# A linear-attention and rational-FFN kernel: the third token tile goes through three quarters of the inner units ahead of the last quarter of the first two

## The chip, the core and the metric

The kernel runs on one core of a Trainium2 chip. The metric is the time of one execution in device microseconds, as the median of several runs. An execution's span, from its first to its last instruction, is what the profiler shows; the time is a little longer than the span.

## What is computed

```python
# linear attention, 4 x 8 heads, 768 steps, 48 wide
for t in range(S):
    cur = einsum('bhd,bhe->bhde', u * k[t], v[t])
    y[t] = einsum('bhd,bhde->bhe', r[t], state + cur)
    state = w[None, :, :, None] * state + einsum('bhd,bhe->bhde', k[t], v[t])
x = y.transpose(0, 2, 1, 3).reshape(3072, 384)
# feed-forward, 384 -> 2048 -> 384, with a rational activation
h = x @ w_in
P = a[0] + a[1] * h + a[2] * h**2 + a[3] * h**3
Q = 1 + |b[0]| * |h| + |b[1]| * h**2
out = (P / (Q + 1e-6)) @ w_out
```

`r`, `k`, `v` are float32; the weights `w_in` (384 x 2048) and `w_out` (2048 x 384) come as float64 and are turned into float32 on the chip.

## The kernel before, in words

**Tiles.** The 3072 tokens are 24 blocks of 128, block n being time chunk n // 4 of batch n % 4. Two blocks are a pair in the attention and a token tile of 256 in the feed-forward: 12 tiles. The 2048 inner units are 16 pieces j of 128. A *slice* s is one tile with two neighbouring j (`JG`), so eight slices are a tile; slices are numbered in the order in which they run, by the list `SL`.

**One slice.** TensorE makes `h` (`f1`, L644: three float32r products, high with high, low with high, high with low; for tile 0 alone, `FULL`, one float32 product per chunk, L650). ScalarE (ACT) makes |h| (L692), two squares (L698, L703), a logarithm (L708) and an exponential (L712), which is 1/Q. VectorE (DVE) makes P's first factor (L716), the high part of the activation (L722), and two steps towards its low part (L726, L732); the low part's product `lo` (L736) is done by GpSimd (POOL) or by DVE, which for the first 20 slices the order table says (`DYN`). Then TensorE multiplies high and low parts with `w_out` into `o` (`f2`, L654 to L656), 12 matmuls a slice.

**Weights.** The weights are 28 pieces (12 of `w_in`, named `i<quarter>_<chunk>`, 16 of `w_out`, named `o<j>`). SP loads a piece's raw words (L374) into one of few staging buffers; ACT does a copy (L392) and two more steps (L380, L383), DVE joins them (L397, out `wfi` or `wfo`), the high part is a cast (L420, `whii`, `whio`), the remainder (L417, `wloi`, `wloo`) is made by POOL or DVE. A quarter of the inner units, four j, needs three pieces of `w_in` and four of `w_out`. Tile 0 reads `wf`, so a remainder of `w_in` is made once tile 0 is through with that quarter.

**Attention.** For a pair, POOL and DVE scale `k` and `r` (L486, L490) and make the bonus (L494 to L508), TensorE transposes (`tk`, `tr`, L513), makes `kv` (L562), `a` (L541) and `y` (L591), DVE masks (`av`, L549), sums the state (L573) and adds `y` (L607). Then `x` is transposed (L619), copied to `xth` (L420) and its remainder made, `xtl` (`xt_lo`, L633).

**What sets the order.** Every step is a task in a table that `build()` and `prologue()` fill; the string `ORDER` lists the tasks by number in the order in which they are issued, each with the letter of its engine where there is a choice (P, D, A, G, S for TensorE, DVE, ACT, POOL, SP), and `w1` is a warming matmul. Each engine runs its own part of this list strictly in order. `placed()` walks through it with the counts of buffers in `CAP`.

**The quarters.** In the kernel before, `NT` = 2 and `NSEG` = 4: tiles 0 and 1 take turns by quarter, (0, first), (1, first), (0, second) and so on, 16 slices; then tile 2 and all later tiles run through whole. At the end of each quarter of tiles 0 and 1 the partial sum in `o` is taken out (`put_out`: the first by L783 or L785 into a buffer `os`, the later ones added to it by DVE, L778), since one `o` per half is all there is.

**The head.** `prologue()` loads `w` (`wraw`), which after two ACT steps (L304, L305) goes through DVE's power scan (L312), and the coefficients `a`, `b`, which take ACT's L260, L261, L265 and L266 and DVE's L264 and L267 to L290, short steps that all activation steps need.

Of the kernel before, what the change touches and what calls it, by code (L numbers as in the profile page):

```python
# [31 lines left out]

PRM = {'NT': 2,
 'NSEG': 4,
# [10 lines left out]
234 0 35 12 13 14 16 18 15 17 20 19 21 5 4 7 22 23 27 44 45 46 47 58 233 59 60 61 1 10 24 25 3 243 30 28 48 236G 11 238G 239 6  # L45
244 62 241 242 29 51 246 245 248G 255 256 26 52 53 54 31 63A 253 254 w1 260 w1 37 38 39 36 55 250G 237G 249G 251 w1 40 262 235
240G 247 259 257A 264A 261 156 157 258A 158 159 41 252G 42D 265 263 267 56D 160 161D 269 268 270 79 80 81 82 83 84A 276 277 279G
280D 285 273 272 271D 274 86 87 275D 88 89 90 2 8 9 72 73 65 66 74 281G 287 85G 64G 266G 282G 289 290 292G 295G 67 75 49A 76 68
69 286D 70D 71G 789 790 791 288D 283 77D 793 93 94 792 803 804 293G 294G 291 278 304 43G 284G 95 794 796 296 96 795 97 797 798
799 800G 309D 805 128 129 130 807 131 132 806 w1 324 100 101 808 102 103 298 300 301D 310 299D 810 104 801 802 78G 323 326G 329G  # L50
297G 327G 114 107 809 115 116 117 303A 811 812 813 814G 305 307 306 308 328D 108 302A 109 110 133A 118 119A 111 312 313 319 314
815 334 318 315 332 336 325 337 339G 342G 343 121 122 123 124 335A 333A 226 227 338 316D 320 321A 317 125 126A 228 340G 345 346D
341G 347 348D 149 150 322 330 351 356 352 229 230 151 816A 152 135 136 137 57G 50G 819 820 821 112D 357 354 98D 153 91D 105D 353
355 138 139 822 154D 823 826 817 818D 824 825 827 828 829 170 350S 171 349S 833 834 837 127G 113G 331G 359 360 361 172 835 173
174 344G 849 850 836 838 365 840 140D 366 212 213 863 864 384 466 142 830G 831 839 841 842 843 99D 832 844D 845 847 851 214 852
215 216 854 865 853 856 855 857 858 848D 143 866 144 868 106G 92G 120G 162G 859 860G 145 146 846D 867 870 147D 869 871 872 385
# [104 lines left out]
def tile_linear_attention_rational_ffn(ctx, tc, r, k, v, w, u, w_in, w_out, a, b, out):  # L161
# [19 lines left out]
    NV = 5  # L181
    TR = HALF + D
    RAW = PRM["RAW"]
    NT = PRM["NT"]
    FULL = PRM["FULL"]
    FULL2 = PRM["FULL2"]
    NTC = 2
# [478 lines left out]
    def opens(s):  # L666
        f, j0, _ = SL[s]
        return j0 == 0 or (f < NT and NT > 1 and j0 % SEG == 0)
# [420 lines left out]
```

## Time and profile before

| | us |
|---|---|
| median of three runs | 544.45 |
| the three runs | 544.45, 541.43, 544.65 |
| the profiled execution | 542.21 |
| its span | 540.4 |
| PE busy | 510.0 (94%) |
| DVE busy | 427.9 (79%) |
| ACT busy | 404.5 (75%) |
| POOL busy | 250.0 (46%) |
| mean granted clock of TensorE | 0.991 |

PE is TensorE's matmuls, DVE is VectorE, ACT is ScalarE, POOL is GpSimd, SP issues the DMAs. "Busy" is the time in which at least one of the engine's instructions was under way; matmuls overlap, so a busy PE need not be at its peak. A row's waits name the engine that was released and the one that released it. A line number is that of the kernel before.

### The profile page before, as it was taken

Reading aid. Unit: us, or ns where it says so; the run is one execution under the profiler, and the core shown is the slowest. Engines: PE = TensorE matmul, PEld = TensorE weight load, DVE = VectorE, ACT = ScalarE, POOL = GpSimd, SP = SyncE. Lnnn points to the kernel's source line nnn. Section 1 sums busy time; section 2 is a strip of 40 time slices with the busy share of each in tenths; the row PEclk is TensorE's granted clock in tenths of the full one; section 3 lists DMA queues with packets and bytes.
Section 4 is the critical chain, followed back from the end, with each engine's and each line's share of the span. In section 5 each row is a group of like instructions: output and inputs, shape, how many; then the busy total and the mean of one; then the engine's idle time right before and its main releaser. Section 6 shows DMA issues by size and latency. Waiting matters only on the chain.

```text
span 540.4 us, 14734 instructions
## 1 busy us (share of the span) xinstructions
PE 510.0 (94%) x6055; PEld 490.7 (91%) x6055; DVE 427.9 (79%) x708; ACT 404.5 (75%) x666; POOL 250.0 (46%) x241
## 2 busy tenths in 40 slices
PE   4758999899999999999999999999999999999995
PEld 2647988899999999999999999999999899999995
DVE  5889999899974887887796868789867785776872
ACT  5789999998864857948963857876785785788782
POOL 3669545384444662551563654235523432222331
PEclk9899999999999999999999999999999999999999
DMA  8967642240022311104304232040031000000001
GB/s 205 267 172 202 183 112 76 79 80 16 16 52 50 79 32 45 31 4 89 81 2 91 52 76 52 2 81 2 2 82 32 1 30 2 2 30 1 29 2 35
DMA packets 88492, 33.46 MB, mean 62 GB/s; under 512 B 81761, under 2 KB 84834, under 8 KB 88418
## 3 DMA queue, kind: packets, MB, share of 16 engines
q1 hardware_dynamic: 88418, 32.46, 25.4%
q8 instruction: 49, 0.80, 0.6%
q14 instruction: 25, 0.20, 0.1%
HBM read 27.73 MB, written 4.72 MB: 60 GB/s over the span
## 4 chain that ended last, share of the span: by engine, by line
PE 76%; DVE 5%; ACT 4%; DMA 1%; issue 1%; POOL 0%; DVEq 0%; POOLq 0%; ACTq 0%; SPq 0%
PE h L644 30%; PE o L654 11%; PE o L656 11%; PE o L655 11%; PE y L591 3%; PE h L650 2%; PE kv L562 2%; PE a L541 2%; PE tr L513 2%; PE tk L513 2%; PE x L619 1%; DVE q L726 1%; DVE g L722 1%; ACT w L698 1%; DVE h L716 1%
## 5 line engine op out<-in xcount | busy, mean ns | idle before, releaser
L736 POOL TENSOR_TENSOR g<-q,z 128x512 fp32r<-128x512 f32 (+1 forms) x92 | 118.5, 1289 | 234.4 <-DVE q L732 142.9
L644 PE MATMUL h<-xth,whii 128*128 128x256 f32 x528 | 151.2, 286 | 0.1
L644 PE MATMUL h<-xtl,whii 128*128 128x256 f32 x528 | 148.0, 280 | 0.0
L644 PE MATMUL h<-xth,wloi 128*128 128x256 f32 x528 | 148.0, 280 | 0.0
L654 PE MATMUL o<-whio,g 128*128 128x384 f32 x384 | 134.5, 350 | 0.0
L656 PE MATMUL o<-whio,g 128*128 128x384 f32 x384 | 130.3, 339 | 1.9 <-DVE g L736 1.9
L655 PE MATMUL o<-wloo,g 128*128 128x384 f32 x384 | 129.9, 338 | 0.0
L698 ACT ACTIVATE w<-q,off,root 128x512 f32<-128x512 f32 (+1 forms) x97 | 75.4, 779 | 48.5 <-DVE q L726 22.5
L644 PEld LDWEIGHTS h<-xth,whii 128*128 128x128 f32 x528 | 99.4, 188 | 1.7 <-DVE q L726 0.9
L644 PEld LDWEIGHTS h<-xtl,whii 128*128 128x128 f32 x528 | 99.5, 188 | 0.0
L644 PEld LDWEIGHTS h<-xth,wloi 128*128 128x128 f32 x528 | 99.4, 188 | 0.0
L722 DVE SCALAR_TENSOR_TENSOR g<-h,sig,z 128x512 fp32r<-128x512 f32 (+1 forms) x97 | 72.1, 743 | 33.7 <-ACT z L712 29.2
L716 DVE SCALAR_TENSOR_TENSOR h<-t,sig,h 128x512 f32<-128x512 f32 (+1 forms) x97 | 71.9, 743 | 15.6 <-ACT t L703 9.7
L703 ACT ACTIVATE t<-h,off,root 128x512 f32<-128x512 f32 (+1 forms) x97 | 74.3, 767 | 6.8 <-PE h L644 6.6
L726 DVE SCALAR_TENSOR_TENSOR q<-w,sig,g 128x512 f32<-128x512 f32 (+1 forms) x97 | 72.2, 744 | 6.3
L656 PEld LDWEIGHTS o<-whio,g 128*128 128x128 f32 x384 | 72.1, 188 | 3.2 <-DVE g L736 2.9
L732 DVE SCALAR_TENSOR_TENSOR q<-h,sig,q 128x512 f32<-128x512 f32 (+1 forms) x97 | 72.0, 744 | 2.7
L654 PEld LDWEIGHTS o<-whio,g 128*128 128x128 f32 x384 | 72.1, 188 | 1.0
L655 PEld LDWEIGHTS o<-wloo,g 128*128 128x128 f32 x384 | 72.3, 188 | 0.1
L692 ACT ACTIVATE q<-h 128x512 f32<-128x512 f32 (+1 forms) x97 | 56.2, 584 | 20.7 <-PE h L644 19.7
L712 ACT ACTIVATE z<-z,lnb 128x512 f32<-128x512 f32 (+1 forms) x97 | 69.7, 719 | 2.2
L708 ACT ACTIVATE z<-w,lnb 128x512 f32<-128x512 f32 (+1 forms) x97 | 66.0, 680 | 6.9 <-POOL g L736 2.6
(141 smaller groups left out, 664.9 us busy)
## 6 DMA issues: line engine op xcount, KB each, us to landing
sti<-in_moe_w_in_dram SPq DMA_DIRECT2D x12, 512.0 KB, 5.1
sto<-in_moe_w_out_dram SPq DMA_DIRECT2D x16, 384.0 KB, 3.8
rh<-in_r_dram SPq DMA_DIRECT2D x24, 192.0 KB, 3.5
kh<-in_k_dram SPq DMA_DIRECT2D x24, 192.0 KB, 4.0
vn<-in_v_dram SPq DMA_DIRECT2D x24, 192.0 KB, 4.4
out_dram<-os SPq DMA_DIRECT2D x24, 192.0 KB, 2.1
vo<-in_v_dram SPq DMA_DIRECT2D x10, 96.0 KB, 3.9
wraw<-in_w_dram SPq DMA_DIRECT2D x1, 1.0 KB, 2.5
```

What stands on the lines that cost most here:

```text
L644: nc.tensor.matmul(o, w_[nm][:, c], x_[:, cc], start=(n == 0), stop=(n == 3 * NCC - 1))
L654: nc.tensor.matmul(o, hi, w_["hi"], start=first, stop=False)
L655: nc.tensor.matmul(o, hi, w_["lo"], start=False, stop=False)
L656: nc.tensor.matmul(o, lo, w_["hi"], start=False, stop=last)
L698: nc.scalar.activation(g["w"], w_, AF.Square, scale=RB, bias=KB)
L703: nc.scalar.activation(g["t"], g["h"], AF.Square, scale=RA, bias=KA)
L712: nc.scalar.activation(g["z"], g["z"], AF.Exp, scale=-1.0, bias=lnb[:, 1:2])
L716: nc.vector.scalar_tensor_tensor(g["h"], g["t"], KAP, g["h"], op0=ALU.add, op1=ALU.mult)
L722: nc.vector.scalar_tensor_tensor(g["hi"], g["h"], c0, g["z"], op0=ALU.add, op1=ALU.mult)
L726: nc.vector.scalar_tensor_tensor(g["q"], g.get("w", g["q"]), qe, g["hi"].bitcast(F32), op0=ALU.add, op1=ALU.mult)
L732: nc.vector.scalar_tensor_tensor(g["d"], g["h"], c0, g["q"], op0=ALU.add, op1=ALU.subtract)
L736: e.tensor_mul(g["lo"], g["d"], g["z"])
```

## The change

`NT` and `NSEG` go, and a list of groups comes in their place: (tile, first quarter, end quarter). Tiles 0 and 1 take turns in the first three quarters (12 slices), then tile 2 runs through the same three quarters in one group (slices 12 to 17), then tiles 0, 1 and 2 each through the last (18 to 23). From tile 3 on all is as it was. Tile 2's sum is therefore taken out twice instead of once. `xth` has three buffers and `xtl` two, where both had two, and `xtl` is made only when it is first written. The order table is written anew for the whole program, from its first task on; so the engines' queues differ in many places, the choice of DVE or POOL included.

```diff
-PRM = {'NT': 2,
- 'NSEG': 4,
+PRM = {'GROUPS': ((0, 0, 1), (1, 0, 1), (0, 1, 2), (1, 1, 2), (0, 2, 3), (1, 2, 3), (2, 0, 3), (0, 3, 4), (1, 3, 4), (2, 3, 4)),
...
 ORDER = """
-234 0 35 12 13 14 16 18 15 17 20 19 21 5 4 7 22 23 27 44 45 46 47 58 233 59 60 61 1 10 24 25 3 243 30 28 48 236G 11 238G 239 6
+0 156 157 w1 7 35 12 13 14 16 15 w1 18 17 20 51 158 159 52 160 3 6 5 4 22 23 27 19 21 w2 29 24 1 25 30 161D 162G 2 245 8 9 53 54
...
+    NXT = {"xth": 3, "xtl": 2}
...
     def xt_lo(n):
         f, q = divmod(n, TB)
+        if q == 0:
+            xts[f].append(at.tile([P, NCC, N1], F32R, tag="xtl", name=f"xtl{f}", bufs=NXT["xtl"]))
...
-    NSEG = PRM["NSEG"]
-    SEG = NJ // NSEG
-    SL = [(f, j, JG) for g in range(NSEG) for f in range(NT) for j in range(g * SEG, (g + 1) * SEG, JG)] if NT > 1 else []
-    SL += [(f, j, JG) for f in range(NT if NT > 1 else 0, NTILE) for j in range(0, NJ, JG)]
+    SEG = NJ // 4
+    PART = [(f, a * SEG, b * SEG) for f, a, b in GROUPS]
+    PART += [(f, 0, NJ) for f in range(len({f for f, _, _ in PART}), NTILE)]
+    SL = [(f, j, JG) for f, a, b in PART for j in range(a, b, JG)]
     SL[-1:] = [(NTILE - 1, j, 1) for j in range(NJ - JG, NJ)]
+    FIRST, LAST = {(f, a) for f, a, _ in PART}, {(f, b) for f, _, b in PART}
...
     def closes(s):
         f, j0, nj = SL[s]
-        return j0 + nj == NJ or (f < NT and NT > 1 and (j0 + nj) % SEG == 0)
+        return (f, j0 + nj) in LAST
+
+    def spare(s):
+        f, j0, nj = SL[s]
+        return "m" if f < 2 and j0 + nj < NJ else "os"
```

What ACT's queue begins with, before (`cp`, `upi`, `upo` are the steps of a weight piece, `sti` and `sto` its raw words of w_in and w_out; `sq` and `cen` lead to the power scan):

```order
L199 ACT_TABLE_LOAD
L304 ACTIVATE sq_88<-wcol_83 112x4
L305 ACTIVATE cen_89<-sq_88 112x4
L392 ACTIVATE cp1_152<-sti0_1_150 128x512
L380 ACTIVATE upi0_1_154<-sti0_1_150 128x512
L383 ACTIVATE upi0_1_154<-sti0_1_150 128x512
```

and now (`beta`, `cabs`, `sqs` and `root` are coefficient steps):

```order
L199 ACT_TABLE_LOAD
L392 ACTIVATE cp17_129<-sto8_127 128x384
L304 ACTIVATE sq_88<-wcol_83 112x4
L305 ACTIVATE cen_89<-sq_88 112x4
L380 ACTIVATE upo8_147<-sto8_127 128x384
L383 ACTIVATE upo8_147<-sto8_127 128x384
L392 ACTIVATE cp2_150<-sti0_2_145 128x512
L260 ACTIVATE beta_86<-coef_84 128x2
L261 ACTIVATE cabs_95<-coef_84 128x6
L265 ACTIVATE sqs_186<-ctmp_96 128x2
L266 ACTIVATE root_93<-sqs_186 128x2
```

The copy of a w_out piece has moved ahead of the two steps on `w`, and the coefficient steps follow right behind the first piece, in front of a second piece's steps.

What DVE's queue has from slice 3's last step to slice 4's, before (`wfo13` and `wloi1_1` are weights, `os` a partial sum taken out):

```order
L732 SCALAR_TENSOR_TENSOR q3_1113<-h3_1051,sig_97,q3_1113 128x512
L417 TENSOR_TENSOR wloi1_1_1165<-wfi1_1_590,whii1_1_977 128x512
L736 TENSOR_TENSOR g3_1161<-q3_1113,z3_1128 128x512
L397 SCALAR_TENSOR_TENSOR wfo13_1193<-cp25_1137,upo13_1188 128x384
L716 SCALAR_TENSOR_TENSOR h4_1119<-t4_1199,sig_97,h4_1119 128x512
L722 SCALAR_TENSOR_TENSOR g4_1203<-h4_1119,sig_97,z4_1195 128x512
L726 SCALAR_TENSOR_TENSOR q4_1186<-w4_1190,sig_97,g4_1203 128x512
L785 TENSOR_SCALAR os1_1_1206<-o1_1_1153,sig_97 128x384
L732 SCALAR_TENSOR_TENSOR q4_1186<-h4_1119,sig_97,q4_1186 128x512
```

and now, from one row ahead of slice 3's last step to one behind slice 4's (`wfi3_1` and `whii3_1` are of the last quarter, `xth2` and `xtl2` are tile 2's input):

```order
L397 SCALAR_TENSOR_TENSOR wfi3_1_1199<-cp22_1169,upi3_1_1171 128x512
L737 SCALAR_TENSOR_TENSOR q3_1120<-h3_1030,sig_97,q3_1120 128x512
L741 TENSOR_TENSOR g3_1166<-q3_1120,z3_1138 128x512
L633 TENSOR_TENSOR xtl2_1209<-x4_1186,xth2_1196 128x3x128
L721 SCALAR_TENSOR_TENSOR h4_1143<-t4_1211,sig_97,h4_1143 128x512
L420 CAST whii3_1_1218<-wfi3_1_1199 128x512
L397 SCALAR_TENSOR_TENSOR wfi2_1_1221<-cp15_1207,upi2_1_1214 128x512
L727 SCALAR_TENSOR_TENSOR g4_1226<-h4_1143,sig_97,z4_1223 128x512
L731 SCALAR_TENSOR_TENSOR q4_1173<-w4_1216,sig_97,g4_1226 128x512
L420 CAST xth2_1196<-x5_1201 128x3x128
L737 SCALAR_TENSOR_TENSOR q4_1173<-h4_1143,sig_97,q4_1173 128x512
L633 TENSOR_TENSOR xtl2_1209<-x5_1201,xth2_1196 128x3x128
```

Tile 2's input and a join of the last quarter stand here now; before, that join came behind slice 8's last step, and `xtl2` behind slice 11's.

## Rows read from the trace of the kernel before

**Rows 1.** The page's view of the span in 40 equal slices (13.5 us each): busy tenths of TensorE (PE) and VectorE (DVE), and the granted clock of TensorE in tenths.
```profile
PE   4758999899999999999999999999999999999995
...
DVE  5889999899974887887796868789867785776872
...
PEclk9899999999999999999999999999999999999999
```

**Rows 2.** The windows view: busy us of each engine in four stretches (in brackets the instructions), then the granted clock, the mean busy share of the DMA engines and GB/s. First the stretch and its length.
```profile
0.00:40.50 40.50, 24.18 (x356) 19.14 (x356) 29.94 (x72) 28.78 (x58) 23.00 (x38) 0.92 0.87 215
40.50:111.00 70.50, 64.79 (x754) 59.18 (x755) 66.69 (x113) 66.94 (x119) 40.99 (x37) 1.00 0.47 125
111.00:164.00 53.00, 51.88 (x535) 50.80 (x533) 47.35 (x72) 41.44 (x66) 27.45 (x25) 1.00 0.20 42
164.00:300.00 136.00, 135.58 (x1930) 132.02 (x1930) 105.17 (x172) 92.85 (x150) 67.99 (x63) 1.00 0.25 53
```

**Rows 3.** The waits view of the stretch from 50 to 115 us, TensorE's rows: who waited for whom, us in total, times, longest.
```profile
PE o L656 <- DVE g L736: 1.9, 2, 1.0
...
PE h L650 <- DVE q L726: 0.7, 1, 0.7
PE h L650 <- DVE wfi L397: 0.6, 1, 0.6
```

**Rows 4.** The chain of waits, merged, in order of time (start us, us, what; x is the number of instructions), from 104 to 174 us.
```profile
104.53 5.45 PE h L650 x24
...
111.03 0.33 PE x L619 x3
...
114.86 7.39 PE h L644 x63
122.26 0.44 PE tr L513 x4
...
173.69 1.07 PE kv L562 x57
```

**Rows 5.** The timeline of VectorE: start us, us, engine, line, operation, out<-in, shapes, in brackets the idle time before it and who ended it. The L732 rows are slice 0's, 11's and 23's.
```profile
5.12 1.23 DVE L312 TENSOR_TENSOR_SCAN pw<-wcol,cen,zero 112x128 f32<-112x128 f32 x3
...
12.34 0.55 DVE L504 TENSOR_REDUCE dt<-m 128x8 f32<-128x384 f32 x1 [1.82 <-POOL m L499]
...
23.18 0.62 DVE L607 TENSOR_TENSOR m<-y,m 128x192 f32<-128x192 f32 x2 [1.31 <-PE y L591]
...
27.64 1.94 DVE L264 TENSOR_SCALAR ctmp<-cabs 128x2 f32<-128x2 f32 x1
...
32.77 0.15 DVE L290 SCALAR_TENSOR_TENSOR lnb<-sig,sqs 128x1 f32<-128x1 f32 x1
...
39.79 0.75 DVE L732 SCALAR_TENSOR_TENSOR q<-h,sig,q 128x512 f32<-128x512 f32 x1
...
103.78 0.69 DVE L397 SCALAR_TENSOR_TENSOR wfi<-cp,upi 128x512 int32<-128x512 int32 x1 [0.95 <-ACT upi L383]
...
110.29 0.75 DVE L732 SCALAR_TENSOR_TENSOR q<-h,sig,q 128x512 f32<-128x512 f32 x1
111.07 0.98 DVE L736 TENSOR_TENSOR g<-q,z 128x512 fp32r<-128x512 f32 x1
...
163.45 0.74 DVE L732 SCALAR_TENSOR_TENSOR q<-h,sig,q 128x512 f32<-128x512 f32 x1
```

**Rows 6.** The timeline of TensorE, the same columns: tile 0's first product in its two halves, the first matmul into `o` behind the last quarter's first products, those of slices 11 and 23, and the last matmul of the program.
```profile
27.18 3.86 PE L650 MATMUL h<-xth,wfi 128*128 128x256 f32 x12
33.98 2.86 PE L650 MATMUL h<-xth,wfi 128*128 128x256 f32 x12 [2.95 <-DVE wfo L397]
...
109.63 0.52 PE L654 MATMUL o<-whio,g 128*128 128x384 f32 x1
...
112.26 0.34 PE L654 MATMUL o<-whio,g 128*128 128x384 f32 x1
...
174.69 0.45 PE L654 MATMUL o<-whio,g 128*128 128x384 f32 x1
...
534.29 0.33 PE L656 MATMUL o<-whio,g 128*128 128x384 f32 x1
```

**Rows 7.** The timeline at the start, the same columns: the second part of SyncE's issue of `wraw`, and ScalarE's (ACT's) first step on `w` and its first copy of a weight piece.
```profile
2.08 0.59 SPq L234 DMA_DIRECT2D wraw<-in_w_dram  x1
...
4.57 0.20 ACT L304 ACTIVATE sq<-wcol 112x4 f32<-112x4 f32 x1 [2.47 <-DVE wcol L301]
...
7.32 0.62 ACT L392 ACTIVATE cp<-sti 128x512 f32<-128x512 f32 x1 [2.31 <-DMA sti<-in_moe_w_in_dram]
```

**Rows 8.** The view of one tile, `sto` (the raw words of a piece of w_out): from the issue of its DMA to the landing, over 16 DMAs.
```profile
DMA to landing us min/median/max: 2.9/3.8/5.5
```

**Rows 9.** The groups view of VectorE between 40.5 and 111 us: line, operation, out<-in, shapes, count | busy us, mean ns of one | idle us before.
```profile
L397 DVE SCALAR_TENSOR_TENSOR wfo<-cp,upo 128x384 int32<-128x384 int32 x10 | 5.5, 547 | 0.1
...
L736 DVE TENSOR_TENSOR g<-q,z 128x512 fp32r<-128x512 f32 x3 | 3.1, 1032 | 0.0
...
L417 DVE TENSOR_TENSOR wloi<-wfi,whii 128x512 fp32r<-128x512 f32 x1 | 1.2, 1223 | 0.0
L633 DVE TENSOR_TENSOR xtl<-x,xth 128x384 fp32r<-128x384 f32 x2 | 1.1, 552 | 0.0
```

**Rows 10.** The windows view of one more stretch, the columns of group 2.
```profile
20.00:30.00 10.00, 7.73 (x86) 6.44 (x87) 7.38 (x14) 5.02 (x14) 7.22 (x8) 0.66 0.98 252
```

More of the change, by code (lines that the diff above doesn't have):

```diff
@@ L49 @@
[L49 to L56, printed above, removed]
@@ L624, in xt_hi @@
         if q == 0:
-            xts[f] = tuple(
-                at.tile([P, NCC, N1], F32 if f in FULL else F32R, tag=s, name=f"{s}{f}") for s in (("xth",) if f in FULL else ("xth", "xtl"))
-            )
+            xts[f] = [at.tile([P, NCC, N1], F32 if f in FULL else F32R, tag="xth", name=f"xth{f}", bufs=NXT["xth"])]
         copy(e, xts[f][0][:, :, ts(q, P)], state[n]["x"])
@@ L779, in put_out @@
             return
-        part = j0 + nj < NJ
-        os_ = at.tile([P, DM], F32, tag="m" if part else "os", name=f"os{f}_{hf}", **({"bufs": NM} if part else {}))
+        tag = spare(s)
+        os_ = at.tile([P, DM], F32, tag=tag, name=f"os{f}_{hf}", **({"bufs": NM} if tag == "m" else {}))
         if e is nc.scalar:
@@ L793, in tile_linear_attention_rational_ffn @@
     CAP = {
-        "g": NGB, "st": 3, "tb": NTB, "ta": 3, "tc": NTC, "m": NM, "ldv": NV, "dt": 2, "os": 2, "xt": 2,
+        "g": NGB, "st": 3, "tb": NTB, "ta": 3, "tc": NTC, "m": NM, "ldv": NV, "dt": 2, "os": 2, "xt": NXT["xth"], "xu": NXT["xtl"],
         "h": 5, "o": 1, "pa": 1, "wi": NWI, "wo": NWO,
@@ L879, in build @@
                 if m not in FULL:
-                    add(("xl", n), lambda e, n=n: xt_lo(n), "D", [("xh", n)], use=[("x", n), ("xt", m), ("m", n)])
+                    add(("xl", n), lambda e, n=n: xt_lo(n), "D", [("xh", n)] + ([("xl", n - 1)] if x else []), new=[] if x else [("xu", ("xu", m))], use=[("x", n), ("xt", m), ("m", n)] + ([("xu", m)] if x else []))
         def used(ps, s, full):
@@ L895, in build @@
                 add(("f1", s, jj), lambda e, s=s, jj=jj: f1(s, jj), "P",
-                    deps + [(win, p0 + cc) for cc in range(NCC)], new=[] if jj else [("h", h)], use=[("xt", f)] + ([h] if jj else []) + used([p0 + cc for cc in range(NCC)], s, full))
+                    deps + [(win, p0 + cc) for cc in range(NCC)], new=[] if jj else [("h", h)], use=[("xt", f)] + ([] if full else [("xu", f)]) + ([h] if jj else []) + used([p0 + cc for cc in range(NCC)], s, full))
             add(("z", s), lambda e, s=s: ew_z(s), "A", [("f1", s, nj - 1)], new=[("ta", ("q", s))], use=[h])
@@ L923, in build @@
                     add(("os", s, hf), lambda e, s=s, hf=hf: put_out(s, hf, e), "D" if some else "AD", [("f2", s, hf), *prv],
-                        new=[] if some else [("os" if done else "m", buf)], use=[("o", so)] + ([buf] if some else []))
+                        new=[] if some else [(spare(s), buf)], use=[("o", so)] + ([buf] if some else []))
                     if done:
@@ L1036, in general @@
                 nc.tensor.transpose(p_[:, ts(c, P)], x.rearrange("t p c -> t (p c)")[:, ts(c, P)], ident)
-            hi, lo = (at.tile([P, NCC, P], F32R, tag="xt" + s_, name="gx" + s_) for s_ in ("hi", "lo"))
+            hi, lo = (at.tile([P, NCC, P], F32R, tag="xt" + s_[0], name="gx" + s_, bufs=NXT["xt" + s_[0]]) for s_ in ("hi", "lo"))
             pv = p_[:, 0:DM].rearrange("p (c t) -> p c t", c=NCC)
```

150 lines of the change are left out of this document (79 added, 71 removed), and 6 rows, old and new, of the table ORDER.

## The prediction

> **What bounds the kernel now.** I read the page first. In the 40 slices the row PE is at nine tenths or more from slice 5 on, while it is lower, and DVE not yet full, before that [rows 1]. So what can be won or lost lies in the first fifth of the span; behind it PE works at a rate that the change does not touch, since it adds no matmul but a few warming ones. Next the windows, cut at three places of the DVE queue: the end of slice 0's last DVE step (40.5 us), that of slice 11 (111.0) and that of slice 23 (164.2). From 40.5 to 111.0 PE is idle for 5.7 of 70.5 us, DVE for 3.8, ACT for 3.6; from 111 to 164 PE is idle for 1.1 of 53, DVE for 5.7 and ACT for 11.6 [rows 2]. So in the middle stage DVE and ACT are as full as PE, and PE is the engine that has gaps. Then the waits between 50 and 115 us: all that PE waited for there was DVE, 1.9 us for the product `lo` (L736), 0.7 for DVE's queue and 0.6 for a join of a weight (L397) [rows 3]. The chain of waits shows the same kind of step: the join of a last-quarter weight ended at 104.47, and at 104.53 tile 0's full-precision products started, which ran for 5.45 us [rows 4, 5].
>
> I therefore use DVE's queue as the clock of the first 111 us. It is strictly in order, and PE's second matmul of slice s can start when DVE has ended that slice's step L732 and somebody has done L736. The row of slice 11 shows it tight: L732 ended at 111.03, L736 on DVE at 112.05, and PE's first matmul of slice 11 into `o` started at 112.26 [rows 5, 6]. From there PE runs to its last matmul, which ends at 534.62, and the span ends 5.8 us later. So
>
> span before = 111.0 (DVE at slice 11) + 1.1 (L736) + 422.5 (PE) + 5.8 (tail) = 540.4; the program's time adds 1.8: 542.2.
>
> The median of the runs shown is 544.45, and these spread from 541.43 to 544.65; a measurement of this kernel tells about 1% from no change. I forecast on the profiled execution, which lies 0.4% below the median.
>
> **The change, step by step.**
>
> *The head.* Two things move. First, in the new order ACT starts with the copy of a w_out piece, which waits for that piece's DMA, and only then takes the two small steps that free DVE's power scan. Before, the scan started at 5.12 and ACT's first copy at 7.32 [rows 5, 7]. SP was through with issuing `wraw` at 2.67, with one load of `r` (about 0.5 us of issue) ahead [rows 7]; now nothing is ahead of it and the piece comes next, at about 2.2 us; such a piece lands 2.9 to 5.5 us after its issue [rows 8], so between 5.1 and 7.7. With 0.5 for the copy and 0.4 for ACT's two steps the scan starts between 6.0 and 8.6; I take 7.0, near the lower end because nothing else is on the DMA queue yet: 1.9 us later. Second, the coefficient steps (L264 to L290), which DVE did at 27.64 to 32.9, are now done before the first tile's attention. That is no extra work, 5.3 us either way, but it puts tile 0's first product back: it started at 27.18, its second half only at 33.98, held up by these very steps [rows 5, 6]. In the new order everything ahead of it includes them, so it starts near 33 and runs through. Both halves end within some 2 us of where they did. DVE's own queue up to slice 0's end has 75 instructions in place of 71, 2.0 us more by the mean durations. Of the 1.9 us late start about 1.0 is left, since the waits that DVE had there, 1.82 on POOL and 1.31 on PE's first attention, are in part filled by the moved steps [rows 5]. So slice 0 ends at 40.5 + 2.0 + 1.0 = 43.5; bounds 41.5 (all waits filled) and 46.
>
> *From slice 0 to slice 11.* DVE has 124 instructions in place of 112. What comes: two joins (L397, 0.55 each), two `xtl` (L633, 0.55) since tile 2 has to be ready by now, two state sums, two bonus sums, one bonus product and one eviction (0.55 to 0.6 each), two casts, two weight remainders net; what goes: one scaling and one product `lo`. By the rows of this stretch that is 5.3 us [rows 9]. DVE took 70.5 us for this stretch before; it sat idle for a part of that waiting for ACT, 0.95 us in one place [rows 5]. The new order converts earlier and may lose such waits: I take 1.0 off, bounds 0 and 2.3. So 70.5 + 5.3 - 1.0 = 74.8, and slice 11 ends at 118.3 instead of 111.0.
>
> *What PE has done by then.* That is the point of the change. Ahead of slice 11's second matmul PE had done two slices of tile 0's last quarter (24 records, 5.1 us from the first at 104.53 to the next matmul at 109.63). Now it has done three slices of tile 2 (54 matmuls at 0.117, from 63 in 7.39 us: 6.35), four transposes of 0.44 (1.76), one `kv` (1.07) and one `x` (0.33): 9.5 us [rows 4, 6]. So PE is 4.4 us further on, and what is left behind slice 11 is 422.5 - 4.4 = 418.1 us. PE's stalls behind 112 us stay as they were: they are other waits, of attention, and I have no row that makes them longer or shorter; I allow 2 us either way.
>
> *The cost of the cover.* The wait on the last quarter's join does vanish, as tile 2 stands in front of it. But the conversions are not spread out: up to slice 11, DVE does 28 of the 28 joins where it did 27. The work that fills the cover, tile 2's attention and its split, is itself DVE work, and so the queue that was late is late by more (7.3 us) than PE has gained (4.4).
>
> *Behind slice 11.* To slice 23 DVE has 75 instructions in place of 71, four more of them products `lo` taken from POOL: 2.0 us more. DVE ended L732 of slice 23 at 164.2 and PE only came to that slice's `o` at 174.69, 62.4 us behind slice 11's [rows 5, 6]. Now DVE ends it at 164.2 + 7.3 + 2.0 = 173.5 at the latest and its `lo` takes 1.0 more; PE comes there at 119.4 + 62.4 - 4.4 = 177.4. About 3 us of cover are left, so this costs nothing; if that goes, the time grows one for one with it. The two added partial sums of tile 2 (0.6 us each on DVE) lie here too, beside PE's matmuls. The tail, the last two slices, is the same row for row.
>
> Sum: 118.3 + 1.1 + 418.1 + 5.8 = 543.3 us of span, 2.9 more than before, and with 1.8 around it 545.1. I say 545.0. Own range of this case 542 to 549: slice 0 between 41.5 and 46, waits 0 to 2.3, PE's stalls 2 either way.
>
> *A price that varies.* The same DVE instruction between two SBUF tensors takes very different times: L736 averages 1.03 us on DVE in this stretch and the weight remainder L417 1.22, and the coefficient step L264, on two elements, took 1.94, with POOL busy in the whole of it [rows 5, 9]. I have charged the moved steps by the short durations (about 0.55); with the long ones the stretch to slice 11 would cost 3 us more. The Trainium skill has a rule for this: the page GPSIMD Engine Reference, section "8. Key points", says that GpSimd shares its SBUF interfaces with VectorE and that these contend where a DVE instruction has two SBUF inputs or runs in a two-port mode. By that rule the sum would be 548; the trace agrees for L264 and leaves it open for the others.
>
> **The rivals.**
>
> *The cover works (16%).* PE never waits in the stage that was starved, because DVE's waits on ACT and DMA were what made it late, and the new order has none. For it: PE's idle time there is only waits on DVE, and 5.7 us of it would go. Against it: DVE was idle for only 3.8 of the 70.5 us, so it has no room for 5.3 us more work. Time: 542.2 - 5.7 = 536.5; with the loss of the head of 1 us, 537.5.
>
> *Even (20%).* The change does not do what it says: all joins stand before slice 11 as before, so the order of PE's work is only exchanged, and DVE, with its 2.3 us of waits gone and a head no later, loses just what PE gains. 43.5 - 2 + 70.5 + 5.3 - 2.3 = 115.0 at slice 11, and 540.0 of span: 541.8, say 542.
>
> *The head falls behind (19%), slower than before.* Place: tile 0's first product, now at 33 us. PE has long gaps ahead of it, and the clock granted in 20 to 30 us was 0.66 on average, that is half (1.2 GHz) for some 7 us after such gaps; the first half of the product took 3.86 us, the second, at full clock (2.4 GHz), 2.86 [rows 6, 10]. If the piece lands late (scan at 8.6, 1.6 us more) and all of the product runs at half the clock (24 records of 0.21 more, 5.1 us), slice 1 comes 5 to 6 us later; about 5 of it reach slice 11, as DVE is full from there on. Time: 545 + 5 = 550. It decides as soon as slice 0 ends behind 47 us. The page TensorE: Matmul & The Clock Gate, section "What's actually happening", of the Trainium skill says that the clock is halved by default and that activity releases it, which speaks for this rival: the trace shows it in that one stretch.
>
> **How the numbers follow.** Forecast 45%, even 20%, the cover works 16%, the head falls behind 19%. Faster by over 1% (below 539) is the cover's case: 0.16. Slower by over 1% (above 549.9) is the head's and the forecast's upper edge: 0.22. Within 1%: 0.62. The range goes from 538.5, which takes in the cover's milder half, to 551.
>
> **What would show it.** Right: DVE ends slice 0's L732 near 43.5 and slice 11's near 118; no PE wait on a weight join between 50 and 115 us, but waits on L736 (DVE or POOL) of tile 1 and 2; PE's idle time from slice 0 to slice 11 not below 5.7 us; PE's last matmul near 537. Wrong: slice 11 by 113 or earlier, then the cover works and DVE had the room; slice 23's `lo` ending later than PE comes to it, then DVE binds longer than I said; a low granted clock between 30 and 45 us, then it is the head.

## The result, and the profile after

The changed kernel takes 547.59 us by the median of 20 runs (544.09 to 551.56), the kernel before 544.55 by the median of 20 (541.43 to 546.87): a ratio of 1.006, with a 95% interval of 1.0039 to 1.0081, or some 3 us more. The ratios are worked out over all runs and can differ a little from those of the medians. The forecast was 545.0, with a range of 538.5 to 551 and "within 1%" as the likeliest case. The number that the profile shows is another one: its execution took 551.56 us, a span of 549.8, the longest of the 20, with the lowest mean granted clock of them (0.972; the others have 0.978 to 0.999). So what it shows over 547.6 is not in every run, and I use it for where time goes, and medians for how much.

The page of the changed kernel, the slices that answer to [rows 1]: PE, DVE, the granted clock, and the busy share of the DMA engines.

```profile
PE   3777798999999999999999899999999999999995
...
DVE  5779779999879888978796859778786768885782
...
PEclk9769979999999999999999999999999999999998
DMA  8976914450004220215231130132000000000001
```

Slices are 13.7 us here. In the old order slice 1 alone was below nine tenths of the clock (8); now slices 1 and 2 are at 7 and 6, and slice 5 is at 7 again, behind a slice 4 in which the DMA engines were at nine tenths. The windows, cut where DVE ended slice 0's, 11's and 23's last step, answer to [rows 2] (us of each engine, in brackets the instructions, clock, DMA share, GB/s):

```profile
0.00:44.80 44.80, 27.89 (x368) 22.41 (x368) 31.81 (x76) 29.42 (x59) 20.39 (x35) 0.81 0.81 192
44.80:122.90 78.10, 70.36 (x854) 64.24 (x855) 69.98 (x125) 70.85 (x123) 45.22 (x41) 0.96 0.55 138
122.90:178.40 55.50, 55.50 (x542) 53.89 (x541) 48.38 (x76) 42.26 (x65) 23.91 (x21) 1.00 0.12 25
178.40:300.00 121.60, 121.22 (x1766) 117.35 (x1765) 100.28 (x166) 84.66 (x136) 56.96 (x51) 1.00 0.25 53
60.00:70.00 10.00, 6.98 (x218) 6.43 (x217) 6.15 (x16) 6.99 (x12) 1.60 (x2) 0.92 0.99 236
68.40:75.20 6.80, 6.28 (x21) 5.38 (x21) 5.19 (x11) 3.69 (x7) 0.00 (x0) 0.50 0.29 107
```

DVE has 125 instructions in the second stretch where it had 113, and takes 78.1 us for it in place of 70.5. PE's idle time there went up, from 5.7 us to 7.7, and after it there is none at all up to 178.4. What PE waited for, from 45 us to 180, the rows of 0.5 us and more (the view of [rows 3]):

```profile
PE y L591 <- issue: 3.0, 1, 3.0
PE h L644 <- DVE q L731: 1.6, 1, 1.6
PE a L541 <- DVE q L737: 1.0, 1, 1.0
PE y L591 <- DVE av L549: 0.8, 1, 0.8
PE o L656 <- DVE g L741: 0.7, 1, 0.7
PE tk L513 <- DVE wfo L397: 0.7, 1, 0.7
```

The wait of a first product on a weight join is gone, as the change means it, and the waits for `lo` fell from 1.9 to 0.7. On top stands a row that the kernel before does not have in this size: 3.0 us of "issue", time in which PE waited for nothing that the profile shows. DVE's timeline beside [rows 5] (the first scan, the first and the last coefficient step, slice 0's last step, the wait behind PE's standstill, slices 11 and 23):

```profile
6.26 0.86 DVE L312 TENSOR_TENSOR_SCAN pw<-wcol,cen,zero 112x128 f32<-112x128 f32 x2
...
11.66 0.15 DVE L264 TENSOR_SCALAR ctmp<-cabs 128x2 f32<-128x2 f32 x1
...
15.02 0.15 DVE L290 SCALAR_TENSOR_TENSOR lnb<-sig,sqs 128x1 f32<-128x1 f32 x1
...
44.02 0.75 DVE L737 SCALAR_TENSOR_TENSOR q<-h,sig,q 128x512 f32<-128x512 f32 x1
...
69.30 0.89 DVE L607 TENSOR_TENSOR m<-y,m 128x192 f32<-128x192 f32 x3 [2.92 <-PE y L591]
...
122.11 0.74 DVE L737 SCALAR_TENSOR_TENSOR q<-h,sig,q 128x512 f32<-128x512 f32 x1
122.89 0.69 DVE L741 TENSOR_TENSOR g<-q,z 128x512 fp32r<-128x512 f32 x1
...
177.71 0.74 DVE L737 SCALAR_TENSOR_TENSOR q<-h,sig,q 128x512 f32<-128x512 f32 x1
```

and PE's beside [rows 6] (tile 0's first product, the standstill, the wait at 86.4, slice 11's second matmul, the second standstill):

```profile
33.91 5.99 PE L650 MATMUL h<-xth,wfi 128*128 128x256 f32 x18
...
42.18 1.56 PE L650 MATMUL h<-xth,wfi 128*128 128x256 f32 x6
...
68.92 0.34 PE L591 MATMUL y<-vn,av 64*64 64x48 f32 x2 [3.02 <-issue]
...
71.27 7.28 PE L650 MATMUL h<-xth,wfi 128*128 128x256 f32 x24
...
86.41 0.36 PE L644 MATMUL h<-xth,whii 128*128 128x256 f32 x1 [1.57 <-DVE q L731]
...
125.04 0.34 PE L654 MATMUL o<-whio,g 128*128 128x384 f32 x1
...
314.07 0.46 PE L654 MATMUL o<-whio,g 128*128 128x384 f32 x1 [1.83 <-issue]
```

The reader is to see four things. The scan began at 6.26 in place of 5.12, and tile 0's first product at 33.91; its first 18 matmuls took 5.99 us, most of them at half the clock (1.2 GHz), which lasted from 20.6 to 37.7. From 65.9 to 68.9 PE stood still with 2 of the 64 small products of `y` left to issue; half clock followed from 68.4 to 75.2, and 24 matmuls of tile 0 took 7.28 us where [rows 4] had 5.45. DVE waited 2.92 us for those two products. And behind 86.4 us no wait of PE is longer than 0.4 us (0.38, at 212.5) until a second standstill of 1.83 us at 312, again with half clock behind it (3.4 us).

In both standstills a block of PE's own instructions was on its way, in the middle of the first (65.9 to 68.9) and up to 0.4 us into the second (312.2 to 314.1): the packed trace has it from 66.08 to 67.54 and from 311.73 to 312.61, and PE went on 1.4 and 1.5 us after these landings. The page counts these blocks as queue 8, 49 of them with 0.80 MB, one for some 250 of PE's instructions. The DMA view from 65.5 to 69 us (queue, packets, MB, share of the 16 engines) shows what the first block stood among:

```profile
q1 hardware_dynamic: 1361, 0.74, 95.2%
q8 instruction: 1, 0.02, 2.6%
```

### The profile page after: what moved, and what is told of

Same layout as the page of the kernel before. It is cut to its first block, busy times and chain, and to the rows that moved or that the text cites. A ratio compares the mean times of both kernels' runs of the same rounds, so it can differ in the third digit from the quotient of the medians.

```text
span 549.8 us, 14789 instructions
## 1 busy us (share of the span) xinstructions
PE 517.3 (94%) x6059; PEld 496.5 (90%) x6059; DVE 434.3 (79%) x730; ACT 406.5 (74%) x663; POOL 235.5 (43%) x222
## 4 chain that ended last, share of the span: by engine, by line
PE 88%; DVE 5%; ACT 2%; issue 2%; DMA 1%; POOL 0%; SPq 0%; DVEq 0%; ACTq 0%; POOLq 0%
PE h L644 33%; PE o L654 12%; PE o L655 12%; PE o L656 12%; PE y L591 5%; PE h L650 5%; PE kv L562 2%; PE a L541 2%; PE tr L513 2%; PE tk L513 2%; PE x L619 2%; DMA sto<-in_moe_w_out_dram 1%; DVE pk L318 1%; DVE q L731 1%; DVE g L727 1%
## 5 line engine op out<-in xcount | busy, mean ns | idle before, releaser
L741 POOL TENSOR_TENSOR g<-q,z 128x512 fp32r<-128x512 f32 (+1 forms) x89 | 115.4, 1297 | 223.2 <-DVE q L737 149.3
```

What stands on the lines that cost most here:

```text
L741: e.tensor_mul(g["lo"], g["d"], g["z"])
```

## The experiments

The theories: (A) PE runs out of instructions where a block's border falls into a long row of small products, and the half clock behind it doubles the price; (B) DVE's queue is the clock, as I had forecast; (C) the head's late start passes through. All medians stand against the kernel before in the same job, which had 544.6 to 545.5.

**head_back.** One entry of the order: 157, ACT's first copy, moves behind 13, the steps that free the scan.

```diff
-0 156 157 w1 7 35 12 13 14 16 15
+0 156 w1 7 35 12 13 157 14 16 15
```

> The changed kernel with one edit in ACT's row: the first copy of a w_out piece stands behind the two small steps that free DVE's power scan, no longer ahead of them. Theory C (the head's late start passes through): the first scan at about 4.5 in place of 6.26, slice 0's L737 1 to 1.8 us earlier than 44.8, 546 by the median against 547.6. Theory A and the rest: the scan is earlier, but the wait for the coefficient step and PE's first transposes take it up, slice 0 within 0.5 us, 547 to 548.

Measured: 544.85 us (12 runs), ratio 1.0014 (0.9986 to 1.0043): of the loss of 3 us nothing clear is left, though this interval and that of the change (1.0039 to 1.0081) just touch. DVE's and PE's timelines:

```profile
4.43 0.17 DVE L311 COPY pw<-cen 112x4 f32<-112x4 f32 x1 [0.51 <-ACT cen L305]
...
38.56 0.75 DVE L737 SCALAR_TENSOR_TENSOR q<-h,sig,q 128x512 f32<-128x512 f32 x1
```

```profile
29.90 4.53 PE L650 MATMUL h<-xth,wfi 128*128 128x256 f32 x18
```

The scan's first step came 1.75 us earlier, tile 0's first product 4.0, and slice 0's end 5.5 (39.3 in place of 44.8): the 18 matmuls took 4.53 us, and the half clock lasted 3.4 us where it had lasted 17.1. So a start 1.8 us late went with three times itself at slice 0 in this pair of profiles, and with 2.7 us by the medians. The pair is an extreme one: these are the lowest granted clock of the changed kernel's runs (0.972) and nearly the highest of head_back's (0.996), while the mean over all runs is 0.989 in both. The profiles of lighter and spaced, whose heads are the changed kernel's, have slice 0's end at 43.3 and 44.9, and groups_back, with head_back's head, at 41.9, so the difference is anything from 1.4 to 5.6 us. Theory C held, in that the late start passes through; that half clock multiplies it is seen in this pair and not in the runs as a whole. From slice 0 to slice 11 DVE needed 75.2 us, not 78.1.

**before_copy** puts the same defect into the kernel before:

```diff
-234 0 35 12 13 14 16 18 ... 22 23 27 44 45 46
+234 0 44 45 35 12 13 14 16 18 ... 22 23 27 46
```

> The kernel before with the head's defect alone: the load of the first w_in piece is issued ahead of the recurrence's w, and its copy on ACT stands ahead of the two small steps that free DVE's power scan. No other instruction moves. Theory C (what the changed kernel lost, it lost by this in the head): the scan starts at 6.5 to 7.5 in place of 5.12, slice 0 ends 2 us or more later than 40.5, and the median is 547 to 549 against 545.4. Theory B (the head's start is filled up by waits that were there, the middle is what costs): slice 0 within 1 us, 545 to 546.

Measured: 550.62 us (5 runs), ratio 1.0108 (1.0074 to 1.0142). DVE's timeline:

```profile
8.30 0.17 DVE L311 COPY pw<-cen 112x4 f32<-112x4 f32 x1 [3.77 <-ACT cen L305]
...
45.90 0.75 DVE L732 SCALAR_TENSOR_TENSOR q<-h,sig,q 128x512 f32<-128x512 f32 x1
```

The w_in piece landed later than the one of w_out (its load stands behind those of `w`, not ahead of them as I had written), the scan began 3.3 us later, slice 0 ended 6.1 later, and the time grew by 5.2, beyond the 547 to 549 that I expected: again more than the delay itself.

**coef_late** and **before_coef** test the other thing that moved in the head, the coefficient steps (8 and 9), in either order.

```diff
 coef_late, from head_back:
-... 2 245 8 9 53 54 ...  49A 82 271A ...  300 275D 789
+... 2 245 53 54 ...  49A 82 8 271A ...  300 275D 9 789
 before_coef, from the kernel before:
-... 27 44 45 46 47 58 ... 30 28 48 236G ...  89 90 2 8 9 72
+... 27 44 2 45 46 47 8 58 ... 30 28 48 9 236G ...  89 90 72
```

> The kernel head_back with the coefficient steps (L260 to L290) put back to where the kernel before has them on ACT and DVE, behind tile 0's attention. As predicted (they cost the same either way): tile 0's first product starts 3 to 4 us earlier than 29.9, its second half or slice 0's first ACT steps wait for the coefficients, slice 0 ends within 1.5 us of 39.3, and the median within 1.5 us of 544.85. If their early place was what fills the head: slice 0 over 1.5 us later and 546.5 or more; if it was in the way: 543 or less.

> The kernel before with the coefficient steps (L260 to L290) in the early place that the changed kernel gives them: the load of the coefficients behind the first weight piece, their ACT steps behind the first piece's, their DVE steps behind the first join. Nothing else moves. In the changed kernel's head the early place was worth 3.9 us by the medians (coef_late against head_back). If the same holds here: tile 0's first product has no gap of 3.3 us in its middle any more, slice 0 ends 2 to 4 us earlier than 40.5, and the median is 541 to 543.5 against 545.4, which would mean that the regrouping is worth nothing beside it. As the prediction had it (5.3 us either way): 544.5 to 546.

Measured: coef_late 548.79 us (ratio 1.0068, 1.0038 to 1.0099), 3.9 more than head_back; before_coef 542.96 (0.9975, 0.9947 to 1.0004), 1.6 less than before, an interval that just holds no change; its slice 0 ended at 39.4, 1.2 us earlier than before, where I had expected 2 to 4. The first and the last of the moved steps in their late place (coef_late):

```profile
26.81 0.96 DVE L264 TENSOR_SCALAR ctmp<-cabs 128x2 f32<-128x2 f32 x1
...
34.20 0.15 DVE L290 SCALAR_TENSOR_TENSOR lnb<-sig,sqs 128x1 f32<-128x1 f32 x1
```

Early, L264 took 0.15 us and the whole group 3.5 (11.66 to 15.17); in the kernel before it took 1.94 and the group 5.3 [rows 5]; late in the new order 0.96 and 7.5, with a wait and other steps between. In the early place POOL was idle beside it: its 8.39 us of idle time ended only with this step, as POOL's timeline of the changed kernel shows:

```profile
11.83 1.00 POOL L417 TENSOR_TENSOR wloo<-wfo,whio 128x384 fp32r<-128x384 f32 x1 [8.39 <-DVE ctmp L264]
```

In the kernel before POOL was at work beside it throughout. That fits the rule of the Trainium skill that I had cited (GPSIMD Engine Reference, "8. Key points"), that GpSimd and VectorE share SBUF interfaces. No run here keeps the place and changes POOL alone, so this is the likely reason and not a shown one. My expectation that the place costs nothing failed in the new order; in the old one it is open.

**lighter** and **heavier** test theory B by the engine letters alone.

```diff
 lighter, from the changed kernel (L494, L494, L417 x3, L741 x2 to POOL)
-326D 339D 134D 120D 169D 844D 934D
+326G 339G 134G 120G 169G 844G 934G
 heavier, from the kernel before (L494 x2, L417 x4, L499 x2, L486, L490 to DVE)
-326G 339G 120G 134G 169G 155G 329G 342G 340G 341G
+326D 339D 120D 134D 169D 155D 329D 342D 340D 341D
```

> The changed kernel with seven steps given from DVE to POOL in place (two bonus products L494 of tile 2, three weight remainders L417, two products lo L741, of slices 3 and 9): by the rows 0.55 for the first five and 0.94 for lo on DVE, together 4.6 us less on DVE before slice 11 ends. Theory B (DVE's queue is the clock up to slice 11, one for one): slice 11 ends some 4 us earlier, 543 to 545 by the median against 547.6. Theory A (the two standstills of PE and the half clock behind them): these stay, 546.5 to 548.5, and the row 'issue' of about 3 us near 66 us is in the profile again.

> The kernel before with ten steps given from POOL to DVE in place (L494, L499 of the two blocks of tile 2, one L486, one L490, four remainders L417, all ahead of slice 11): 0.55 each by the short rows, up to 1.2 by the long ones, so 5.5 to 8 us more on DVE up to slice 11. Theory B (one for one, less waits on POOL that go): slice 11's L732 at 115 to 118 in place of 111.0 and 548 to 550.5 by the median against 544.55. Theory A (DVE's load does not set the time here): within 1 us of 544.55.

Measured: lighter 554.56 us (1.0213, 1.0162 to 1.0263), heavier 554.01 (1.0172, 1.0138 to 1.0207). PE's waits, 60 to 130 us in lighter and 40 to 125 in heavier:

```profile
PE o L656 <- POOL g L741: 6.2, 3, 3.7
PE y L591 <- issue: 2.8, 1, 2.8
```

```profile
PE h L644 <- DVE wloi L417: 5.4, 1, 5.4
PE tk L513 <- DVE q L732: 2.6, 1, 2.6
```

In lighter DVE was 3.8 us earlier at slice 6 (95.0 against 98.8), 1.4 of them at slice 0 already, when only one of the seven steps had come. So from slice 0 to slice 6 it gained 2.4, as theory B says. Then PE waited 6.2 us for `lo` on POOL, 5.0 of them for the two products that I had given to it, for POOL's queue is in order too and sat behind a wait: the load was only moved to the next queue. In heavier DVE was 6 us later at slice 6, and PE then waited 5.4 us for one remainder: 8.6 us more in all, over what B gave. So in the old order DVE's load does pass through, and more than one for one where a step that PE needs stands behind it.

**spaced.** Two rows of PE, for pair 2 (the other is pair 8's):

```diff
-a2 ys2 f1(3,0) y2 f1(3,1) f1(4,0) f1(4,1) f1(5,0)
+a2 f1(3,0) f1(3,1) ys2 f1(4,0) f1(4,1) y2 f1(5,0)
```

> The changed kernel with five steps of PE's row moved apart: tile 2's two state products (y from st) and its last attention step stand one half-slice of F1 (L644) later each, and the same for pair 8 (kernel line L541, L591 near 310 us). Nothing else changes but nine short DVE steps that follow them. Theory A (PE ran out of instructions: in the profile of the changed kernel it stood still for 3.02 us at 65.9 and 1.83 us at 312.2 with nothing that it waited for, each time while a 16 KiB block of its own instructions was on its way, in the middle of three or four groups of 64 small products in a row; and the granted clock halved behind it): both 'issue' rows are gone or under 1.2 us, no half clock behind 45 us, DVE ends slice 11 at 116 to 119 in place of 122.9, and the time is 541.5 to 545 by the median, against 547.6 for the change as it stands. Theory B (DVE's queue alone, as predicted: slice 11 late because DVE is full): DVE has the same steps, so 547 to 549, with or without the issue rows.

Measured: 552.42 us (1.0126, 1.0093 to 1.016). PE's timeline:

```profile
67.77 1.95 PE L591 MATMUL y<-st,rt 48*64 48x48 f32 x62 [2.49 <-DVE wfo L397]
73.75 4.74 PE L650 MATMUL h<-xth,wfi 128*128 128x256 f32 x12 [4.03 <-DVE q L737]
```

The standstill at 312 is gone. The one near 65 moved to the start of `ys2`, with a block on its way from 65.01 to 66.33 (the view puts its 2.49 us down to an old join), and `y2`, now later, held up DVE, for which PE then waited 4.03. An attempt that does not tell A from B; what it shows is that `y2` must not come later.

**fetch_shift** and **shift_late** add 88 warming matmuls (176 instructions) to head_back, in PE's gaps, so that all later borders fall elsewhere:

```diff
 fetch_shift, from head_back:
-15 w1 18 17 20 ...  255 241 237G ...  285 88
+15 w1 18 w50 17 20 ...  255 241 w18 237G ...  285 w20 88
 shift_late, from head_back:
-255 241 237G ...  267 268 ...  285 88 ...  298 299D ...  305
+255 241 w14 237G ...  267 w14 268 ...  285 w28 88 ...  298 w12 299D ...  w20 305
```

> The kernel head_back (the changed kernel with ACT's first copy behind the two steps for the scan; 544.85 us median, slice 11 ended at 114.5 in its profile) with 88 warming matmuls more on PE, in three gaps of the first 28 us (50, 18 and 20). They add no work that anything waits for, and they move all later PE instructions by 176 against the borders of the 16 KiB blocks in which they come. Theory A (PE stands still where such a border falls at the start of a long group of small products: matmuls number 855 and 3778 in every run of the changed order, 2.0 to 3.0 and 1.5 to 1.8 us): both standstills are gone from the rows, slice 11 ends at 112 to 113, and the median is 541.5 to 543.5. If the standstill is nothing that can be moved: the rows stay at the products of y near 60 and 303 us and the time is 544 to 545.5. If the warming matmuls come in the way of the head: slice 0 later than 39.3 and over 545.5.

> The kernel head_back with the same 88 warming matmuls as fetch_shift, but only 14 of them ahead of tile 0's attention and 74 behind it, in gaps of PE up to its first F2. In fetch_shift the two standstills behind 45 us were gone or short (0.7 us), but 68 matmuls ahead of the first attention put a block's border into it: a new standstill of 2.68 us at 23.2 us, and slice 0 ended at 42.7 in place of 39.3. Theory A (borders of the instruction blocks, which can be placed): no standstill over 1 us anywhere behind 20 us, slice 0 at 39 to 40, slice 11 at 113 to 114.5, median 540 to 542. If the warming matmuls delay the first product: slice 0 over 41 and 542.5 or more.

Measured: fetch_shift 542.47 us (0.9956, 0.9932 to 0.998), shift_late 540.47 (0.9927, 0.9898 to 0.9956), each of 12 runs. PE's waits in shift_late from 40 us to the end:

```profile
PE h L645 <- DVE q L732: 1.9, 2, 1.6
PE o L657 <- DVE g L742: 1.1, 1, 1.1
PE y L592 <- DVE av L550: 0.8, 1, 0.8
PE tk L514 <- DVE wfo L398: 0.7, 1, 0.7
PE y L592 <- issue: 0.5, 1, 0.5
```

Of the standstills 0.5 us is left. In the changed kernel, head_back, lighter and coef_late they stood at the same two matmuls, numbers 855 and 3778, at times from 60 to 66 and 304 to 318 us; with the borders moved they are gone from both places. fetch_shift put a border into tile 0's attention instead and stood still there for 2.68 us at 23 us, and was still faster than head_back by 2.4. Theory A holds for where PE stands still. The warming matmuls also keep PE busy ahead of the first product, and the mean granted clock over the runs is 0.995 in shift_late, against 0.989 in head_back, so the clock may have a share in its 4.4 us. It does not explain all: in fetch_shift the mean is 0.985. From 0.984 to 0.986 head_back's runs took 544.4 to 545.5 us and fetch_shift's 541.2 to 543.2, and at 0.994 head_back's took 548.2 and 548.6, shift_late's 540.2 and 542.2.

**after_shift** and **before_shift** ask the same of the changed kernel as it stands, and of the old order with the early coefficients.

```diff
 after_shift, from the changed kernel:
-255 241 237G ...  267 268 ...  285 88 ...  298 299D ...  305
+255 241 w14 237G ...  267 w14 268 ...  285 w28 88 ...  298 w12 299D ...  w20 305
 before_shift, from before_coef:
-263 267 56D ...  298
+263 267 w12 56D ...  w43 298
```

> The changed kernel as it stands (ACT's first copy still ahead of the scan) with the 88 warming matmuls of shift_late, 14 ahead of tile 0's attention and 74 behind it. In the pair without the late scan they were worth 4.4 us by the medians (head_back 544.85, shift_late 540.47). Theory A (the standstills at matmuls 855 and 3778 and the half clock behind them are what the forecast left out; without them its sum of 545 holds): the standstills behind 45 us are gone, the stretch from slice 0 to slice 11 falls from 78.1 to 74.5 to 75.5, and the median is 543 to 545. If the late scan alone made the difference: 546.5 or more.

> The kernel before_coef (the order before with the coefficient steps early; 542.96 median) with 55 warming matmuls more, 12 behind tile 0's attention and 43 in the gap behind its first product, which moves all later PE instructions by 110 against the borders of their blocks; in its profile PE stood still for 1.3 us at 160 us with 3.4 us of half clock behind it. What it tells: the regrouping with head and borders mended (shift_late, 540.47) against the old grouping with both mended. If the regrouping is worth the 4.4 us of PE's work that it puts ahead of slice 11, less the 4.3 us of DVE's that it adds there: within 1 us of shift_late, 540 to 541.5. If the old grouping is as good without its added DVE work: 539.5 or less. If the regrouping is what won: 542 or more.

Measured: after_shift 541.59 us (0.9941, 0.992 to 0.9963), before_shift 541.71 (0.9942, 0.9918 to 0.9967). after_shift in windows, 20 to 40 us and from slice 0 to slice 11, and the changed kernel's own 20 to 40 us:

```profile
20.00:30.00 10.00, 8.12 (x276) 7.53 (x277) 8.65 (x17) 8.22 (x17) 6.96 (x8) 1.00 0.89 210
30.00:40.00 10.00, 9.29 (x120) 7.81 (x118) 9.46 (x19) 8.47 (x15) 4.33 (x6) 1.00 0.85 211
41.00:115.60 74.60, 68.20 (x859) 62.07 (x857) 69.97 (x125) 70.48 (x123) 45.99 (x41) 1.00 0.57 144
```

```profile
20.00:30.00 10.00, 8.13 (x231) 7.42 (x226) 6.80 (x13) 7.26 (x15) 5.78 (x7) 0.53 0.89 218
30.00:40.00 10.00, 8.70 (x33) 7.25 (x34) 7.51 (x16) 6.09 (x12) 3.67 (x4) 0.62 0.66 169
```

6.0 us less than the changed kernel, though the scan is as late as there (its first step at 6.46). The clock was at its full 2.4 GHz from 19.5 us, where its record begins, up to the last matmuls; slice 0 ended at 41.0, and slice 11 came 74.6 us later. Against shift_late the late scan now costs 1.1 us, with intervals that overlap: with no half clock behind it, at most a small loss is left. And with head and borders mended in both, the new grouping (shift_late) and the old (before_shift) are 1.2 us apart, with intervals that overlap: unclear.

**groups_back** is head_back with the old grouping; the order table follows it from slice 14 on, and nothing else is planned anew.

```diff
-... (0, 2, 3), (1, 2, 3), (2, 0, 3), (0, 3, 4), (1, 3, 4), (2, 3, 4))
+... (0, 2, 3), (1, 2, 3), (0, 3, 4), (1, 3, 4))
```

> The kernel head_back with the grouping of the kernel before: the last quarters of tiles 0 and 1 stand ahead of tile 2, which is done in one run of eight slices and has no partial sum (two ACT steps and two DVE steps fewer). All conversions, attention steps and their places are those of the changed kernel; only from slice 14 on PE's row falls behind by what has to be ready first (weight remainders of the last quarter). As predicted (ahead of slice 11's second matmul PE has done 9.5 us of work by the new grouping and 5.1 by the old, and the joins are not the bound any more): PE waits 2 to 5 us between 100 and 125 us for remainders or slices of the last quarter, and the median is 546.5 to 549. If the regrouping itself is worth nothing: 544 to 545.5. If the old grouping is better by the partial sum it saves: 543 or less.

Measured: 571.67 us (1.0507, 1.0476 to 1.0537). PE's waits from 90 to 200 us:

```profile
PE h L644 <- POOL wloi L417: 9.8, 2, 8.6
PE h L644 <- DVE q L737: 6.8, 2, 6.4
```

Tile 1's last quarter needs remainders that the new order makes only at 132 us, and PE stood for 9.8 us before them; 27 us in all. The new order's conversions and its grouping belong together; what this run prices is not the regrouping but how far its conversions were put back.

## Why the prediction was right, and where it was not

The class and the range held, and the centre was 2.6 us low. Most of that is the base: I forecast on the profiled execution of the kernel before (542.2), which lies 2.3 us under its median of 20. The difference itself, 2.8 us forecast (545.0 against 542.2) and 3.0 measured, agrees by luck: it was to be DVE's load less PE's gain, and head_back, with all of that load, does not have it. By its own steps:

- *The scan starts at 7.0 (6.0 to 8.6).* Right: it began at 6.26, near the lower end, 1.1 us later than before and not 1.9.
- *Of the late start about 1.0 us is left at slice 0.* Wrong in size: 5.5 in the profiles of the changed kernel and head_back, 2.7 by the medians. I had counted waits that fill up, and left the clock to a rival. In this execution the rival's sign came: half clock from 20.6 to 37.7 us, and so 0.62 on average from 30 to 40, within the 30 to 45 us that I had named. It was wrong in price (550 by 5 us at slice 11) and in the point from which it decides: slice 0 ended at 44.8, not behind 47, and the loss was there. For the medians the clock is no answer: the changed kernel's runs have 0.989 on average, those of the kernel before 0.985 in each of the four later series.
- *The coefficient steps cost the same in either place.* Wrong in the new order: the early place is worth 3.9 us by the medians, and 3.7 at slice 0 (39.3 against 43.0), of which up to 2.6 can be the spread of one head (groups_back has 41.9). In the old order it is worth 1.6, not clear of nothing. The two errors have opposite signs, and so it is luck that slice 0's 44.8 lies near my 43.5.
- *From slice 0 to slice 11, 74.8 us.* Right: 75.2, 74.7 and 74.6 in head_back, shift_late and after_shift. In the changed kernel it took 78.1. The 3 us between go with PE's standstill at 65.9, for which DVE waited 2.92, and the 6.8 us of half clock behind it; no term of mine has either. The standstill alone does not cost its full length there: head_back has one of 2.0, with no half clock behind, DVE waited 1.81 for it, and its 75.2 are only 0.6 above after_shift's. The short durations were the right ones for most of what moved: joins of `w_out` took 0.55, `xtl` 0.55, state sums 0.55. The long ones, by which the stretch would have cost 3 us more, stayed for L742 in after_shift (1.02).
- *Slice 11 is where PE waits for DVE.* Wrong. PE came to slice 11's second matmul at 125.04, and its `lo` had ended at 123.58; up to 178.4 PE's last wait over 0.21 us was at 86.4. To that extent the cover works, as the rival had it: nothing waits for a join or for `lo` of tile 2 behind that point, and of the waits on `lo` that I named as a sign only 0.7 us came. But the 5.7 us that this was to save were not to be had, since PE was idle for more before 86 us than the old order was (7.7 against 5.7 us, as my sign of not below 5.7 had it; 6.4 in after_shift). The sum from slice 11 still came out within 2 us (122.9 + 425.0 = 547.9, and 549.8 measured), but by luck, since DVE and PE are only 1.5 us apart there. In the difference lie the second standstill, 1.83 us, and 3.4 us of half clock behind it, less two waits of the old order that are gone (1.11 at 162, 1.01 at 424).
- *Behind slice 11 nothing binds.* Right: PE came to slice 23 at 182.26, POOL's `lo` ended at 179.89, a cover of 2.4 us where I had 3. The tail was 5.7 us, as before. The last matmul ended at 544.2, not 537, by what came earlier and the second standstill.

What I did not have is PE's standstill for want of instructions, with the half clock that follows. The kernel before has it too, 2.2 us in three pieces in its profile, under "issue", and I gave them no term. The step that failed, then, is the one by which "PE's stalls behind 112 us stay as they were", with "no row that makes them longer or shorter", and the same silence about the stretch ahead of it: a new order of PE's row moves its small products against the borders, and these stalls with them, from 2.2 us to 4.8 in the two profiles. Beside it failed the term of the late start, 1.0 us, which measured 2.7.

Not settled: runs of one kernel spread over 3 to 7.5 us. In the kernel before the mean granted clock orders them: in the four later series its runs go from 545.4 to 547.7 us at 0.979 down to 541.2 to 542.0 at 0.992 and 0.993. In the changed kernel it does not (one run at 0.999 took 548.06, one at 0.989 544.09, three at 0.994 549.7 to 550.8), and what makes its runs at a full clock differ so, no run here shows. At 0.992 and 0.993 shift_late's runs took 540.8 to 542.3 us, no less than the kernel before at that clock; so the 4 us by which its median is ahead of the kernel before may be the clock, and no gain of the regrouping is shown. And one control is missing: a whole block of warming matmuls, which leaves the borders about where they were. It would tell the borders from any other effect of the warming matmuls.

## What to carry to other kernels

When an order is changed by hand or by a planner, look first at what moved in the first microseconds of each queue: here one copy, put ahead of two 0.2 us steps, cost 2.7 of the 3.0 us that the whole change lost. Count PE's idle time under "issue" too, and if it falls in a row of small products, move the borders with a few matmuls in a gap before planning anything anew: 88 of them were worth 4 to 6 us, by the borders and the clock together. And where DVE and POOL are both nearly full, giving work from one to the other moves the wait rather than taking it away.

## What the runs showed of the hardware

A block of PE's instructions that comes late stopped PE for up to 3.0 us. In all 24 rows of "issue" over 0.4 us in the 14 profiles, PE went on 1.2 to 1.6 us after a block had landed, and 2.3 to 3.4 us after it began to come (66.08 + 1.46, and 68.92; 302.78 + 1.19, and 305.47 in head_back). An estimate from these rows says why it is the small products: 64 of them with their weight loads are 128 of the some 250 instructions of a block, and two such groups ran in 2.1 us (61.42 to 63.49 in the changed kernel). Groups in a row thus use up a block in less time than the next one needs. Ahead of the two standstills in the changed kernel PE had run some 445 and 485 matmuls and weight loads since the block before began to come, where some 250 are usual; that number alone does not tell, for the kernel before had 437 at 317.5 us and stood still for no more than 0.2. Whether busy DMA engines make a block late, no run tests: they were busy around both blocks, 95% and all of the time, but the second took 0.88 us, as short as any in that profile. The Trainium skill, "Runtime: NRT & Kernel Launch", section "Instruction fetch mechanics", says that blocks of 256 instructions are fetched ahead by the engine's own queue and that crossing a border is "mostly hidden". The size agrees; the hiding does not hold here for groups of 64 small products in a row.

The granted clock fell to half behind both standstills of the changed kernel (3.02 and 1.83 us). It did not fall behind head_back's of 2.0 us at 60 us, nor at the same matmul behind 2.73 in coef_late, 2.83 in lighter and 2.63 in groups_back; so how long PE stood still does not decide it. A late start in the head can cost more than itself: 1.75 us cost 2.7, and 3.3 us cost 5.2, by the medians.
